# A spectral filter beside a gated feed-forward layer on one core: the first four tiles for slabs 0 and 1 alone, row parts of the weights, and stages moved in a hand-written order

## The chip, the core and the metric

The kernel runs on one core of a Trainium2 chip. A core has a matrix engine (PE) that multiplies a stationary operand of up to 128 x 128 by a moving one of up to 512 columns and adds into PSUM, a vector engine (DVE), a scalar engine with function tables (ACT), a general engine (POOL) and a queue engine (SP) that here only issues transfers. ACT and POOL issue transfers too. Each engine works through its own list in order and waits for the others through semaphores. The metric is the time of one execution in microseconds on the device, the median of several runs.

## What is computed

The input x has 2048 rows of 640 values. Its rows are normalised (mean 0, variance 1). From the normalised rows two things are made: a filter in the two-dimensional frequency domain, and a gated feed-forward layer with weights of 640 x 1536, 640 x 1536 and 1536 x 640. The result is x plus the product of both.

```
xn = _layernorm(x, axis=-1)
X  = rfft2(xn) ; X = X * (w_r + 1j * w_i) ; s = irfft2(X).astype(bfloat16)
B  = (gelu(xn @ w_gate) * (xn @ w_up)) @ w_down
return x + s * silu(B)
```

## The kernel before, in words

**Slabs and groups.** The 2048 rows are 16 slabs of 128 (slab n1 holds the rows n1, n1 + 16, ...), and four slabs are a group. `X[:, n1, :]` is a slab with its rows on the partitions. For the feed-forward layer a slab is transposed into `XG` (`xnT[g]`), 5 chunks of 128 features by 512 columns for a group. Wg, Wu hold the first two weights as 5 chunks by 1536 columns, and 128 of these columns are a tile t (12 tiles). Wd is the third weight.

**One piece of the first half of the layer** (`ffn_piece`, line 826): 5 matmuls with a tile of Wg or Wu as the stationary operand, some columns of `XG` as the moving one, into a bank of PSUM (`psg` or `psu`, two banks of each). Then ACT makes gelu of psg into `ge` (line 837), or DVE multiplies psu by `ge` into `UT` (line 839). The second half multiplies UT by Wd: `down_third` for groups 0 and 3, and for groups 1 and 2 fourteen `product`s of six matmuls with sums of blocks prepared on DVE (`w_sum`, `u_sum`).

**The order is written out by hand.** `back` (from line 1000) is a list of 144 places, each a piece of PE work; `put(s, f, ...)` hangs further work behind place s, and the last loop emits place after place. What is emitted on one engine runs there in that order. Places 0 to 15 are tiles 0 to 7 of group 0, 16 to 35 the rest of group 0, 36 to 71 group 1 (24 pieces and 12 places of products), 72 to 107 group 2, 108 to 143 group 3.

**The start.** `build` first issues transfers: slabs 0 and 1 (line 84), then Wu in pairs of tiles with slabs 2 and 3 between, and so on, all on SP and all at once (lines 94 to 106); Wg's first six tiles go out on ACT (line 231). DVE makes constants (lines 224 to 330), the last of them `a_y` (line 272). For each slab, `bn_half` twice and `bn_join` give mean and variance (lines 189, 195), a reciprocal root follows (`root_act` on ACT for slab 0, `root` with DVE's add and POOL's power for the others), and `norm` normalises in place (line 218). `slab_Tparts` transposes a slab on PE in two parts of 3 and 2 chunks and copies each from PSUM (line 995), one on DVE and one on ACT. `warm_pe(21)` stands ahead of the first transposes: matmuls of `ones` (256 columns) that nothing reads (line 588). After `root_act`'s root the table for gelu is loaded (line 215).

At place 0 slab 0 goes through tiles 0 and 1 of Wg (`GG`), slab 1 is normalised and transposed, then slab 0 goes through tiles 0 and 1 of Wu (`UU`). Place 1 does both for slab 1. Places 2 to 7 are tiles 2 to 7 for both slabs (256 columns), places 8 to 15 tiles 0 to 7 for slabs 2 and 3, and from place 16 on a piece has 512 columns. Slab 2 is transposed behind place 4, slab 3 within place 7.

**The filter.** Slabs are turned by DMA (`slab_T` with 2, line 539), folded on DVE, transformed by PE (`slab_S1`, `slab_D`) and stored to `ZDR` in DRAM. The middle stage starts when all of ZDR is written: `load_B2` (place 56, line 603) loads it in another layout, ten transfers for five bands of rows, two each. It works in 11 bursts. `s2_step(b)` at place `sb + AT[b]` does three things: PE makes `px` of burst b (line 628); PE makes `pu` of burst b - 1 (line 657); DVE and ACT sort the `pu` into RX (line 672), from where it is stored to `UDR`. Between px and pu stand ACT's copy `xs` (line 640) and DVE's two products with the filter's weights W1, W2 (line 644). `px`, `pu` and later `pv`, `pd` share two PSUM tiles. The last stage loads UDR (`load_V` at place sb + 24), gathers a few columns on POOL (line 713), transforms back (`slab_S1i`, `slab_Di`: lines 735, 762), recombines on DVE, and `finish` multiplies by silu's result, adds x and stores.

With sb = 67 the first burst's px stands behind place 67, within group 1's products.

Of the kernel before, what the change touches and what calls it, by code (L numbers as in the profile page):

```python
# [13 lines left out]
ALU = mybir.AluOpType  # L14
# [62 lines left out]
def build(nc, env):  # L77
# [5 lines left out]
    def load_x(n0, n, eng=nc.sync):  # L83
        eng.dma_start(out=X[:, n0:n0 + n, :], in_=xv[:, n0:n0 + n, :])

    def load_w(k, t0, t1, eng=nc.sync):
        f0, f1 = t0 * P, t1 * P
        eng.dma_start(out=(Wg, Wu)[k][:, :, f0:f1], in_=(wgv, wuv)[k][:, :, f0:f1])

    def load_gu(t0, t1):  # L90
        for k in range(2):
            load_w(k, t0, t1)

    load_x(0, 1)
# [9 lines left out]
    load_x(8, 4)  # L104
    nc.sync.dma_start(out=Wd, in_=B_w_down.rearrange("(t p) d -> p t d", p=P))
    load_x(12, 4)

# [104 lines left out]
    def root_act(n1):  # L212
        rstd[n1] = c1("rst0")
        nc.scalar.activation(out=rstd[n1], in_=mva[n1 // 4][:, n1 % 4, 1:2], func=ACT.Abs_reciprocal_sqrt, bias=eps)
        nc.scalar.activation(out=warm, in_=negpi, func=ACT.Gelu_apprx_tanh)

# [5 lines left out]

    ones = gtile([256], BF16)
    nc.vector.memset(ones, 1.0)
# [100 lines left out]

    fwd_consts()
    vt_iota(0)
    stats(0)
    bn_half(1, 0)
# [254 lines left out]
    def warm_pe(n):  # L584
        if not warm_bank:
            warm_bank.append(bank(0))
        for _ in range(n):
            nc.tensor.matmul(warm_bank[0][:, 0:256], lhsT=ones[:, 0:P], rhs=ones, start=True, stop=True)

# [250 lines left out]

    def ffn_part(g, t, h):
        for k in range(2):
            ffn_piece(g, t, k, h * 256, h * 256 + 256)

# [126 lines left out]

    def ffn_slab(j, tk):
        for t, k in tk:
            ffn_piece(0, t, k, j * P, j * P + P)

    GG, UU = ((0, 0), (1, 0)), ((0, 1), (1, 1))

    def run(*items):
        for it in items:
            it[0](*it[1:])  # L980

    PARTS = ((0, 3), (3, 5))

# [4 lines left out]
    def slab_Tparts(n1):  # L988
        if n1 == 0:
            xnT[0] = slot(0, 5, 512)  # L990
        for (a, b), ev in zip(PARTS, (nc.vector.tensor_copy, nc.scalar.copy)):
            pt = psB.tile([P, 5, P], BF16, tag="b")
            for c in range(a, b):
                nc.tensor.transpose(out=pt[:, c, :], in_=X[:, n1, c * P:(c + 1) * P], identity=ident)  # L994
            ev(out=xnT[0][:, a:b, n1 * P:n1 * P + P], in_=pt[:, a:b, :])
        done.add(("T", n1))

    NP = 8
    STR = (1, 2)
    back = [(run, (ffn_slab, 0, GG), (norm_parts, 1), (slab_Tparts, 1), (vt_iota, 1), (ffn_slab, 0, UU),  # L1000
             (inv_consts, 0), (inv_consts, 1)),
            (run, (ffn_slab, 1, GG + UU), (stats, 2), (root, 2, 1))]
    for h in range(2):
        for t in range(0 if h else 2, NP):
            back.append((ffn_part, 0, t, h))
        if h == 0:
            back[-1] = (run, (ffn_piece, 0, NP - 1, 0, 0, 256), (slab_Tparts, 3), (ffn_piece, 0, NP - 1, 1, 0, 256))
    for g in range(4):
# [12 lines left out]
    def put(s, *item):  # L1021
        plan[s].append(item)

    put(1, inv_rest)
    put(2, norm, 2)
    put(3, bn_half, 3, 0)
    put(4, bn_half, 3, 1)
    put(4, bn_join, 3)
    put(4, root, 3, 1)
    put(4, slab_T, 2, 1)  # L1030
    put(5, norm, 3)
    for g in range(5):
# [4 lines left out]
    for k in range(3):  # L1037
        put(9, ft_phase, 0, k)
    for k in range(4):
        put(7 + 2 * k, stats, 4 + k)  # L1040
    put(13, root, 4, 4)
    put(13, shift, 4, 4)
    for k in range(3):
        put(13, ft_phase, 1, k)
    put(12, tinv_mask, 0)
    put(14, tinv_mask, 1)
    for k in range(4):
# [133 lines left out]
```

## Time and profile before

| what | value |
|---|---|
| median of 3 runs | 193.46 us (193.43 to 193.47) |
| the profiled execution's own time | 193.65 us |
| its span (first to last recorded instruction or transfer) | 191.9 us |
| HBM read, written | 19.03 MB, 7.88 MB |
| DVE, ACT, POOL busy | 79%, 69%, 28% of the span |

A profile is of one execution. Times in it are microseconds from the start of the span. "Busy" is the time in which an engine works on an instruction; the matmuls of PE overlap, so that their ends are modelled, and PE's weight loads (PEld) run beside them. The chain of waits is followed back from the last instruction: at each step to what released it. In a timeline row stand start, duration, engine, line of the kernel, operation, output and inputs, shapes, count, and in brackets how long the engine had been idle before and what ended that. In the table by windows stand the stretch, its length, busy time and count of PE, PEld, DVE, ACT and POOL, the granted clock of PE, the mean busy share of the DMA engines and GB/s. A row of the DMA view has the transfer, the issuing queue, count, size and the median time from issue to landing.

### The profile page before, as it was taken

How to read it: one execution, taken by the hardware profiler on the slowest of the kernel's cores; microseconds unless marked ns; L12 is line 12 of the kernel's file. 1: busy time of each engine (PE TensorE's matmuls, PEld its weight loads, DVE VectorE, ACT ScalarE, POOL GpSimd, SP SyncE). 2: the span in 40 equal slices, each digit the busy share in tenths (PEclk: the TensorE clock that was granted, in tenths of full speed). 3: DMA queues.
4: the chain of work that ended last, by engine and by line, in shares of the span. 5: the costliest groups of instructions: out<-in, count | busy, mean ns of one | idle time of the engine just before them, and what ended most of it. 6: DMA issues, size and time to landing. Idle time of an engine off the chain costs nothing.

```text
span 191.9 us, 4068 instructions
## 1 busy us (share of the span) xinstructions
PE 186.1 (97%) x1453; PEld 115.6 (60%) x1469; DVE 150.9 (79%) x364; ACT 131.9 (69%) x241; POOL 53.9 (28%) x91
## 2 busy tenths in 40 slices
PE   7999999999999999999999999999999999999993
PEld 5788854677655665566543334347775555556772
DVE  6787889899799889846978677685445898888973
ACT  4658557957878778536697878634989776876622
POOL 4458768999040200000000000002030134150400
PEclk9999999999999999999999999999999999999999
DMA  6999999948889994249996444149900084778842
GB/s 164 300 329 360 370 332 170 172 99 318 178 165 191 211 300 120 78 111 230 223 108 123 106 103 103 42 107 273 266 5 0 0 117 111 152 153 213 121 174 62
DMA packets 39700, 32.43 MB, mean 169 GB/s; under 512 B 12928, under 2 KB 37760, under 8 KB 39552
## 3 DMA queue, kind: packets, MB, share of 16 engines
q1 hardware_dynamic: 35888, 27.91, 58.6%
q0 software_dynamic: 1824, 3.28, 9.4%
q10 hardware_dynamic: 1968, 0.98, 1.9%
q8 instruction: 11, 0.18, 0.4%
q14 instruction: 9, 0.07, 0.1%
HBM read 19.03 MB, written 7.88 MB: 140 GB/s over the span
## 4 chain that ended last, share of the span: by engine, by line
PE 95%; DMA 2%; DVE 1%; issue 1%; SPq 0%; ACT 0%
PE psu L832 27%; PE psg L832 27%; PE psg L967 7%; PE psg L933 7%; PE psu L967 6%; PE psu L933 5%; PE pu L657 2%; PE pd L762 2%; PE pv L735 2%; PE pz L555 2%; PE pd L573 2%; PE px L628 2%; DMA X<-in_A_x_dram 2%; PE pt L994 1%; PE pd L575 1%
## 5 line engine op out<-in xcount | busy, mean ns | idle before, releaser
L832 PE MATMUL psu<-XG,Wu 128*128 128x512 bf16 (+2 forms) x284 | 60.4, 342 | 0.5 <-issue 0.3
L832 PE MATMUL psg<-XG,Wg 128*128 128x512 bf16 (+2 forms) x280 | 60.1, 341 | 0.6
L839 DVE TENSOR_TENSOR UT<-psu,ge 128x512 bf16<-128x512 f32 (+2 forms) x58 | 34.4, 594 | 13.6 <-PE psu L832 8.1
L837 ACT ACTIVATE ge<-psg 128x512 bf16<-128x512 f32 (+2 forms) x58 | 30.3, 523 | 21.3 <-PE psg L832 20.6
L832 PEld LDWEIGHTS <-Wu 128*128 128x128 bf16 x290 | 25.9, 98 | 20.9 <-issue 3.4
L832 PEld LDWEIGHTS <-Wg 128*128 128x128 bf16 x290 | 26.5, 98 | 18.8 <-issue 0.2
L967 PEld LDWEIGHTS <-UT 128*128 128x128 bf16 x204 | 19.1, 98 | 6.9
L813 POOL DMA_DIRECT2D VY<-in_A_x_dram x12 | 10.6, 964 | 26.2 <-ACT W L737 10.5
L713 POOL COPY vr<-VY 128x128 bf16<-128x128 bf16 x2 | 0.6, 291 | 60.2 <-DMA VY<-UDR 60.2
L644 DVE TENSOR_TENSOR RZ<-xs,W 128x960 bf16<-128x960 bf16 (+2 forms) x22 | 13.3, 647 | 4.4 <-ACT xs L640 4.4
L967 PE MATMUL psg<-Wd,UT 128*128 128x320 bf16 (+1 forms) x108 | 15.7, 290 | 0.0
L578 ACT CAST RZ<-pd 128x660 bf16<-128x660 f32 x16 | 11.3, 706 | 5.2 <-PE pd L575 5.2
L189 DVE BATCH_NORM_STATS2 st<-X 128x6 f32<-128x320 bf16 x32 | 14.0, 476 | 0.6 <-DMA X<-in_A_x_dram 0.4
L933 PEld LDWEIGHTS <-UT 128*128 128x128 bf16 x120 | 11.4, 98 | 4.8 <-issue 0.4
L967 PE MATMUL psu<-Wd,UT 128*128 128x320 bf16 (+1 forms) x96 | 13.9, 293 | 0.0
L737 ACT CAST W<-pv 128x640 bf16<-128x640 f32 x16 | 11.1, 691 | 3.1 <-PE pv L735 3.1
L763 ACT ACTIVATE W<-pd 128x640 bf16<-128x640 f32 x16 | 11.3, 706 | 1.5 <-PE pd L762 1.5
L557 ACT CAST GEN<-pz 128x640 bf16<-128x640 f32 x16 | 11.2, 698 | 1.2 <-PE pz L555 1.2
L672 ACT CAST RX<-pu 128x480 bf16<-128x480 f32 (+3 forms) x22 | 10.8, 489 | 1.1 <-DVE RX L672 0.3
L640 ACT CAST xs<-px 128x960 bf16<-128x960 f32 (+2 forms) x11 | 10.3, 933 | 0.0
L207 POOL TENSOR_TENSOR rst<-ve,mhalf 128x1 f32<-128x1 f32 (+1 forms) x6 | 5.5, 913 | 11.5 <-DVE ve L205 11.5
L933 PE MATMUL psg<-X,UT 128*128 128x320 bf16 x48 | 7.8, 300 | 0.0
(202 smaller groups left out, 302.1 us busy)
## 6 DMA issues: line engine op xcount, KB each, us to landing
ZDR<-RZ SPq DMA_DIRECT2D x16, 160.5 KB, 4.1
UDR<-RX SPq DMA_DIRECT2D x10, 240.8 KB, 3.1
B<-ZDR SPq DMA_DIRECT2D x8, 240.8 KB, 5.2
W<-UDR SPq DMA_DIRECT2D x2, 963.0 KB, 9.1
X<-in_A_x_dram SPq DMA_DIRECT2D x3, 640.0 KB, 10.3
Wd<-in_B_w_down_dram SPq DMA_DIRECT2D x1, 1920.0 KB, 14.6
VY<-in_A_x_dram POOLq DMA_DIRECT2D x12, 160.0 KB, 4.3
out_dram<-VY SPq DMA_DIRECT2D x12, 160.0 KB, 2.8
```

The source lines that it names most:

```text
L189: nc.vector.bn_stats(out=st_n[n1][:, k, :], in_=X[:, n1, 320 * k:320 * k + 320])
L557: nc.scalar.copy(out=Zt[n1], in_=pz)
L578: nc.scalar.copy(out=zd.rearrange("p c (q e) -> p c q e", e=10), in_=pd[:, :, 0:330].rearrange("p c (e q) -> p c q e", q=33))
L644: nc.vector.tensor_tensor(out=pp[-1], in0=xs, in1=WT[:, :, h0:h0 + n, l0:l0 + w], op=ALU.mult)
L672: copy(out=out, in_=src)
L737: nc.scalar.copy(out=vs, in_=pv)
L763: nc.scalar.activation(out=parts(eobuf, i, 5)[:, :, n1 - DG[i][0], :], in_=pd, func=ACT.Copy, scale=(2.0 if n1 // 4 in BY_SILU else 1.0) / ...
L832: nc.tensor.matmul(ps, lhsT=WT[:, c, t * P:(t + 1) * P], rhs=xnT[g][:, c, c0:c1_], start=(c == 0), stop=(c == 4))
L837: nc.scalar.activation(out=ges[t], in_=ps, func=ACT.Gelu_apprx_tanh)
L839: nc.vector.tensor_tensor(out=UT[:, t, c0:c1_], in0=ps, in1=ges[t], op=ALU.mult)
L933: nc.tensor.matmul(ps, lhsT=lhs[:, t, :], rhs=rhs[:, t, :], start=(t == 0 and i in (0, 1, 3)), stop=(t == 5), skip_group_check=i in (2, 4, ...
L967: nc.tensor.matmul(ph, lhsT=UT[:, t, j * P:(j + 1) * P], rhs=Wd[:, t, c0:c1_], start=(t == 0), stop=(t == NT - 1))
```

## The change

- The row chunks of the weights can be loaded in parts: `PARTS = ((0, 3), (3, 5))`. ACT issues tiles 0 to 3 of Wg in two parts (before: tiles 0 to 5 in three pairs), SP tiles 0 to 3 of Wu in two parts, then tiles 4 to 7 of each in one transfer.
- Only slabs 0 and 1 are issued at once. Wu's parts stand behind a POOL copy of `a_y` into a cell of Wu; slab 2 and all later loads on SP stand behind a POOL copy of slab 0's mean into a cell of slab 2.
- `warm_pe` uses 128 columns, 38 times, and 4 times behind slab 0's transposes. The statistics' second half of slab 1, its join and its root now stand behind slab 0's normalisation and transposes; slab 1's root is made on ACT (two instructions of DVE and POOL less), and the gelu table is loaded behind it. Both copies of slabs 0 and 1 from PSUM are DVE's.
- `ffn_quad`: one slab (128 columns) through four tiles into one bank, so that one gelu or one product takes 4 x 128 columns; slabs 0 and 1 go through tiles 0 to 3 in this way (places 0 to 3). `ffn_multi`: two tiles of 256 columns into one bank: tiles 4 to 7 for slabs 0 and 1 (places 4 to 7), tiles 0 to 7 for slabs 2 and 3 (places 8 to 15). Slab 2 is transposed within place 6.
- Statistics of slabs 2 to 7 move by one place or so, `inv_consts`, `inv_rest`, norms 2 and 3 and `tinv_mask` move too.
- `sb` is 65 in place of 67: `s2_step`, `load_V`, the gathers and the whole last stage move by two places.

```
-    load_w(1, 0, 2)
-    load_w(1, 2, 4)
-    load_x(2, 1)
-    load_w(1, 4, 6)
-    load_x(3, 1)
-    load_gu(6, 8)
-    load_x(4, 4)
-    load_gu(8, 12)
...
-    for t in (0, 2, 4):
-        load_w(0, t, t + 2, nc.scalar)
+    for part in PARTS:
+        load_w(0, 0, 4, nc.scalar, *part)
...
+    nc.gpsimd.tensor_copy(out=Wu[:, 0, 0:1], in_=ab[4][0])
+    for part in PARTS:
+        load_w(1, 0, 4, nc.sync, *part)
     vt_iota(0)
-    stats(0)
+    bn_half(0, 0)
+    bn_half(0, 1)
+    bn_join(0)
+    nc.gpsimd.tensor_copy(out=X[:, 2, 0:1], in_=mva[0][:, 0, 0:1])
+    load_x(2, 1)
+    load_w(0, 4, 8)
+    load_x(3, 1)
+    load_w(1, 4, 8)
+    load_x(4, 4)
+    load_gu(8, 12)
...
     bn_half(1, 0)
     root_act(0)
...
+    def ffn_quad(k, j, *part):
+        if part[0] == 0:
+            cur["m"] = bank(k)
+        ps = cur["m"].rearrange("p (t w) -> p t w", w=P)
+        for a, b in [PARTS[i] for i in part]:
+            for i in range(4):
+                for c in range(a, b):
+                    nc.tensor.matmul(ps[:, i, :], lhsT=WT[:, c, i * P:(i + 1) * P],
+                                     rhs=xnT[0][:, c, j * P:(j + 1) * P], start=(i + c == 0), stop=(c == 4),
+                                     skip_group_check=True)
+        if part[-1] == 1:
+            multi_out(k, 0, ps, j * P, j * P + P)
...
+    def multi_out(k, t0, ps, c0, c1_):
+        if k == 0:
+            ges[t0, c0] = ge
+            nc.scalar.activation(out=ge, in_=ps, func=ACT.Gelu_apprx_tanh)
+        else:
+            nc.vector.tensor_tensor(out=UT[:, t0:t0 + n, c0:c1_], in0=ps, in1=ges[t0, c0], op=ALU.mult)
...
+    back = [(run, (ffn_quad, 0, 0, 0, 1), (vt_iota, 1)),
+            (run, (ffn_quad, 1, 0, 0), (slab_Tparts, 1), (ffn_quad, 1, 0, 1)),
+            (ffn_quad, 0, 1, 0, 1),
+            (ffn_quad, 1, 1, 0, 1)]
+    for h, k, t0 in ((0, 0, 4), (0, 0, 6), (0, 1, 4), (0, 1, 6)) + tuple((1, k, t) for t in (0, 2, 4, 6) for k in range(2)):
+        back.append((ffn_multi, k, t0, 2, 256 * h, 256 * h + 256))
+    back[6] = (run, (slab_T, 2, 1), (ffn_multi, 1, 4, 2, 0, 256))
+    back[7] = (run, (slab_Tparts, 3), (ffn_multi, 1, 6, 2, 0, 256))
...
+    put(1, stats, 2)
+    put(1, root, 2, 1)
+    put(2, bn_half, 3, 0)
+    put(2, bn_half, 3, 1)
+    put(3, norm, 2)
+    put(3, bn_join, 3)
+    put(3, root, 3, 1)
...
-    sb = 67
+    sb = 65
...
-    warm_pe(21)
+    warm_pe(38)
+    norm_parts(0)
+    slab_Tparts(0)
+    warm_pe(4)
     bn_half(1, 1)
     bn_join(1)
-    root(1, 1)
-    norm_parts(0)
-    slab_Tparts(0)
-    warm_pe(2)
+    root_act(1)
+    gelu_table()
+    norm_parts(1)
```

More of the change, by code (lines that the diff above doesn't have):

```diff
@@ L587, in warm_pe @@
         for _ in range(n):
-            nc.tensor.matmul(warm_bank[0][:, 0:256], lhsT=ones[:, 0:P], rhs=ones, start=True, stop=True)
+            nc.tensor.matmul(warm_bank[0][:, 0:P], lhsT=ones, rhs=ones, start=True, stop=True)
     st_b = {}
@@ L970, in down_third @@
                 gated(g, j, k, ph)
[L972 to L976, printed above, removed]
     def run(*items):
@@ L990, in slab_Tparts @@
             xnT[0] = slot(0, 5, 512)
-        for (a, b), ev in zip(PARTS, (nc.vector.tensor_copy, nc.scalar.copy)):
+        for (a, b), ev in zip(PARTS, (nc.vector.tensor_copy, nc.scalar.copy if n1 > 1 else nc.vector.tensor_copy)):
             pt = psB.tile([P, 5, P], BF16, tag="b")
@@ L1022, in put @@
         plan[s].append(item)
[L1024 to L1031, printed above, removed]
+    put(1, stats, 2)
[5 more added lines that the diff above has]
+    put(3, root, 3, 1)
+    put(3, inv_consts, 0)
+    put(3, inv_consts, 1)
+    put(4, inv_rest)
+    put(5, norm_parts, 3)
     for g in range(5):
@@ L1038, in build @@
         put(9, ft_phase, 0, k)
[L1039 to L1042, printed above, removed]
+    for k, at in enumerate((7, 8, 10, 12)):
+        put(at, stats, 4 + k)
+    put(12, root, 4, 4)
+    put(12, shift, 4, 4)
     for k in range(3):
         put(13, ft_phase, 1, k)
-    put(12, tinv_mask, 0)
-    put(14, tinv_mask, 1)
+    put(16, tinv_mask, 0)
+    put(18, tinv_mask, 1)
     for k in range(4):
```

47 lines of the change are left out of this document (28 added, 19 removed).

## The prediction

> **What bounds the kernel now.** I read the page first, then the chain of waits in order of time, the table by windows, and the timelines of the start and of the stage that the change moves.
>
> ```profile
> span 191.9 us, 4068 instructions
> ...
> PE 186.1 (97%) x1453; PEld 115.6 (60%) x1469; DVE 150.9 (79%) x364; ACT 131.9 (69%) x241; POOL 53.9 (28%) x91
> ...
> PE 95%; DMA 2%; DVE 1%; issue 1%; SPq 0%; ACT 0%
> ```
> ```profile
> 1.17 3.19 DMA X<-in_A_x_dram
> 4.38 0.90 DVE st L189 x2
> ...
> 6.05 0.54 PE pt L994 x5
> 6.84 0.76 PE psg L832 x10
> 7.60 0.28 PE pt L994 x5
> 7.88 0.56 PE psu L832 x10
> ...
> 9.56 0.55 PE psg L832 x5
> ...
> 187.99 0.68 PE psg L967 x12
> ...
> 188.69 0.28 ACT XG L867
> ```
> ```profile
> 6.84:188.67 181.83, 180.76 (x1425) 112.16 (x1440) 145.17 (x327) 128.19 (x235) 51.31 (x81) 1.00 0.71 170
> ```
>
> The reader is to see three pieces: a head of 6.84 us until the first real matmul, a stretch of 181.83 us in which PE is idle for 181.83 - 180.76 = 1.07 us at most, and a tail of 191.9 - 188.67 = 3.2 us behind the last matmul. The idle 1.07 us is not waiting either: the trace holds 1425 matmuls there against 1440 weight loads, and each of the 15 missing records leaves a small hole. So the middle can give nothing back. A change gains if it brings the first matmul forward or drops PE work; anything else can only add a wait. The tail hangs on the last matmuls, which the change leaves alone.
>
> **The head.** The chain shows what the first matmul waits for: the landing of slab 1, two statistics of slab 1, then the normalisation of slab 0.
>
> ```profile
> 1.18 4.55 PE L588 MATMUL psg<-GEN 128*128 128x256 bf16 x21 [1.18 <-DVE eps L229]
> ...
> 2.53 0.14 DVE L272 TENSOR_SCALAR a_y<-pb 128x1 f32<-128x1 f32 x1
> ...
> 4.05 0.21 DVE L195 BATCH_NORM_AGGREGATE mva<-st 128x2 f32<-128x12 f32 x1
> 4.29 0.29 ACT L214 ACTIVATE rst<-mva,eps 128x1 f32<-128x1 f32 x1 [2.08 <-DVE mva L195]
> ...
> 4.60 1.28 ACT L215 ACT_TABLE_LOAD   x1
> ...
> 5.62 0.63 DVE L218 TENSOR_SCALAR X<-X,mva,rst 128x384 bf16<-128x384 bf16 x2
> ...
> 6.43 0.36 DVE L995 COPY XG<-pt 128x384 bf16<-128x384 bf16 x1 [0.18 <-PE pt L994]
> ```
>
> The root of slab 0 is ready at 4.29 + 0.29 = 4.58, yet its normalisation starts at 5.62, because bn_half(1, 1), the aggregate and root(1)'s add stand before it on DVE. The change puts them behind it and leaves bn_half(1, 0) in front, which still waits for the landing at 1.17 + 3.19 = 4.36. Half of the pair's 0.90 later, at 4.83, DVE is free: **-0.79 us**. If X1 landed before the aggregate is done (4.26) it would be -0.9; if the larger pieces of Wg beside it delay it by 0.2, -0.6. I take -0.79, since X1 is issued as before.
>
> What this brings forward meets a slower PE. The 21 warm-up matmuls took 4.55 us, 217 ns for 256 columns, against 0.55 / 5 = 110 ns in the chain's row at 9.56. So 38 of 128 columns take 38 x 108 ns = 4.1 us and end at 5.28, where the transposes are now due (6.05 - 0.79 = 5.26). Three of them feed the first copy; all slow they cost 3 x (108 - 56) = 0.16 us (56 ns is 0.28 / 5 in the row at 7.60). The rate changed between 5.7 and 6.05; I take half, **+0.08**. First matmul: 6.84 - 0.71 = 6.13.
>
> [...]
>
> **PE work.** Tiles 0 to 7 were 40 matmuls of 128 columns (tiles 0, 1 for slabs 0, 1), 60 and 80 of 256; they become 80, 40 and 80. That is 40 x 56 - 20 x 110 ns (56 is 0.56 / 10 at 7.88): **+0.04**. The stage otherwise holds the same matmuls.
>
> **Weights and loads.** Wg leaves on ACT as before, in row parts. Wu's two parts now stand behind a POOL copy of a_y (2.53 + 0.14, so issued near 3.0 instead of 1.64), and X2 with all that follows on SP behind a POOL copy of mva (4.05 + 0.21, near 4.6). POOL is free for the first; before the second it has one iota, long done by then.
>
> ```profile
> 0.00:4.00 4.00, 2.82 (x14) 1.97 (x15) 2.60 (x26) 1.49 (x2) 1.98 (x9) 1.00 0.52 129
> 4.00:8.00 4.00, 3.65 (x37) 2.60 (x36) 3.11 (x12) 2.79 (x7) 0.65 (x1) 1.00 1.15 307
> 16.00:24.00 8.00, 8.00 (x77) 7.10 (x74) 6.63 (x19) 5.60 (x16) 6.54 (x5) 1.00 1.07 367
> ```
> ```profile
> Wu<-in_B_w_up_dram SPq DMA_DIRECT2D x1, 320.0 KB, 5.4
> ```
>
> By 4.0 us 129 GB/s x 4 = 0.52 MB had landed; then 307 GB/s with pieces of 512 B, 367 later with 1 KB and more. In the new order Wu part 1 ends at 1.38 MB: 4.0 + 0.86 / 0.307 = 6.8 at the slow rate (6.3 at 367). Part 2 at 1.64 MB: 7.6 (7.0). Wg 4 to 7 at 2.46 MB: 10.3 (9.3). Wu 4 to 7 at 3.28 MB: 13.0 (11.5). PE asks at 6.13 + 1.12 = 7.25, then 7.25 + 0.67 + 0.28 = 8.2, 6.13 + 80 x 0.056 + 0.28 = 10.9, and 10.9 + 4 x 0.55 + 0.28 = 13.4. All four are in time, by 0.4 to 0.6 us at the worse rate: **0**.
>
> **Statistics, table and narrow evictions.** In the new order DVE makes both copies of slab 0 (5.72 to about 6.25), then bn_half(1, 1), the aggregate, ACT's root, and norm 1 near 7.35; slab 1's transposes can start at 7.78, PE gets to them at 6.13 + 32 x 0.056 = 7.92. The copy behind them ends some **0.05** after PE wants it. gelu_table moves behind root_act(1): it ends near 7.3 + 1.28 = 8.6 where it was hidden before, so the first 512-wide gelu and its product end near 10.
>
> ```profile
> L839 DVE TENSOR_TENSOR UT<-psu,ge 128x512 bf16<-128x512 f32 (+2 forms) x58 | 34.4, 594 | 13.6 <-PE psu L832 8.1
> ```
> ```profile
> 11.27 0.56 POOL L207 TENSOR_TENSOR rst<-ve,mhalf 128x1 f32<-128x1 f32 x1 [1.44 <-DVE ve L205]
> ...
> 11.87 0.45 DVE L218 TENSOR_SCALAR X<-X,mva,rst 128x640 bf16<-128x640 bf16 x1 [0.33 <-POOL rst L207]
> ```
>
> Behind that product DVE's order is stats 2, both halves of slab 3, the second product, norm 2: 10.1 + 1.2 + 0.9 + 0.6 = 12.8, done 12.8 + 0.45 = 13.25, while PE reaches slab 2's transposes at 10.94 + 4 x 0.55 = 13.1. Slab 3 follows over POOL's power (0.56) near 14.75, PE at 14.6. These waits add to 0 (starts overlap by 0.1 each on an engine, which would clear them) to 0.3. I take **+0.10**.
>
> **The middle stage two places sooner.** Everything from the first burst on moves with sb.
>
> ```profile
> 82.94 6.26 SPq L603 DMA_DIRECT2D B<-ZDR  x10
> ...
> 87.74 0.48 DVE L875 SCALAR_TENSOR_TENSOR XG<-th,Tfwd 128x320 bf16<-128x320 f32 x1
> 87.85 0.47 ACT L870 ACTIVATE th<-FT 128x320 f32<-128x320 f32 x1 [0.61 <-DVE FT L947]
> 87.88 0.98 PE L933 MATMUL psg<-X,UT 128*128 128x320 bf16 x6
> ...
> 89.60 0.40 PE L628 MATMUL px<-B,MG 64*64 64x160 bf16 x5
> 90.35 0.97 ACT L640 CAST xs<-px 128x960 bf16<-128x960 f32 x1
> 91.41 1.24 DVE L644 TENSOR_TENSOR RZ<-xs,W 128x960 bf16<-128x960 bf16 x2 [1.52 <-ACT xs L640]
> 92.72 0.58 PE L657 MATMUL pu<-RZ,N 64*64 64x160 bf16 x10
> 94.16 0.35 DVE L672 CAST RX<-pu 128x192 bf16<-128x192 f32 x1
> 94.54 1.03 ACT L672 CAST RX<-pu 128x480 bf16<-128x480 f32 x2
> ```
> ```profile
> B<-ZDR SPq DMA_DIRECT2D x1, 240.8 KB, 4.1
> ```
>
> In the clock of before, px of burst 0 moves ahead of two products, from 89.60 to 87.97. Its second half of B (the second of the ten, issued 0.55 after 82.94) lands at 83.5 + 4.1 = 87.6: 0.4 to spare. Burst 1 now stands among the products, with two of them (6 matmuls of 320 columns each, 0.82 us at the rate of the row at 9.56) between px 1 and px 2, where one tile of 1.1 us stood as well. ACT: xs 0 at 88.4, xs 1 at 91.5 behind the tanh that needs a th buffer back; DVE: burst 0's products to 90.7, three gated writes and an add (0.48 each, less overlap), sort at 92.3; ACT's two copies out of pu 0 then end at 93.7, and PE wants that bank at 93.55. So 0.2 us of wait, at most 0.5, at least 0; **+0.10**. ACT's stores of UDR now stand on SP ahead of slabs 14 and 15's turns, which feed place 108, far behind.
>
> ```profile
> 132.42 0.29 POOL L713 COPY vr<-VY 128x128 bf16<-128x128 bf16 x1 [60.24 <-DMA VY<-UDR]
> ...
> 133.13 0.39 PE L735 MATMUL pv<-Tinv,VY 128*128 128x128 bf16 x4
> ```
>
> The inverse's first gather stood 0.7 us before its use; both move two places, the load by two tiles of 1.1, the use by two products, so its cover grows by 0.5: 0.
>
> **Sum:** -0.79 + 0.08 + 0.04 + 0 + 0.05 + 0.10 + 0.10 = -0.42. The profiled execution took 193.65 (span 191.9 and 1.75 around it), so 193.23; the runs' median, 193.46, lies 0.19 lower: **193.04 us**.
>
> **Rivals.**
> Waits eat the head: 0.3 in the early norms and 0.5 in the middle make the sum +0.18: 193.6. For it, the reckoning as it stands shows 0.45 of waits; against it, the overlap of starts.
> Weights late: if the gate on Wu delays by issue and not by bytes, part 1 lands 5.4 (the row of Wu's first load) after 3.0, at 8.4, and PE stands 8.4 - 7.25 = 1.15: -0.42 + 1.15 = +0.73, **194.2, slower**. It decides once part 1 lands after 7.25 + 0.42 = 7.7. Against it, the 5.4 held other queues' bytes.
> [...]
> The middle stands longer: if B lands 1.2 later than reckoned, its 0.4 of cover is gone and PE waits 0.8 in place of the 0.10: 193.7.
> The change doesn't do what it says: X1 lands 0.7 later beside Wg, and nothing is gained at the head: 193.7.
>
> **How the numbers follow.** Forecast 0.54, waits 0.17, late weights 0.11, slow PE 0.05, middle 0.08, X1 0.05. A measurement tells 0.2% (0.39 us) from no change. Of the forecast's own range, 192.65 (no wait at all: -0.79 + 0.04) to 193.3, about 0.44 lies under 193.07 and 0.10 above. Without the middle's wait or with a sooner X1 0.06 of the waits' case lies under it too: faster 0.50. Same: 0.10, 0.11 of the waits, 0.04 of the middle and X1: 0.25. Slower 0.25. The range for 8 in 10 runs from 192.55 (X1 at 4.26, no waits) to 194.0.
>
> **What would show it.** Right: first matmul at 6.0 to 6.3 and the last 0.3 to 0.6 sooner; norm of slab 0 at 4.83 on DVE; PE holes of 0.1 to 0.2 us before slab 3's transposes and before pu of burst 1, none before Wu's or Wg's first use. Wrong: X1 landing after 4.6, PE idle at 7.25, 8.2, 10.9 or 13.4 with a DMA as releaser, ten first matmuls in over 0.8 us, or holes between 130 and 150 us.

## The result and the profile after

| | median of 6 runs | lowest to highest | profiled execution | its span |
|---|---|---|---|---|
| before | 193.47 us | 193.42 to 193.73 | 193.65 | 191.9 |
| after | 194.33 us | 194.14 to 194.65 | 194.14 | 192.1 |

The ratio is 1.0035, with an interval of 1.0025 to 1.0046: slower by 0.86 us, where 0.42 less was forecast, and outside the range (192.55 to 194.0). The kernel before was timed again beside the changed one, so its median is of six executions here.

The page of the changed kernel: span, busy times, and the shares of the chain of waits.

```profile
span 192.1 us, 4116 instructions
...
PE 186.1 (97%) x1492; PEld 117.5 (61%) x1508; DVE 151.3 (79%) x358; ACT 130.5 (68%) x230; POOL 51.7 (27%) x92
...
PE 94%; DMA 2%; ACT 1%; issue 1%; DVE 1%; SPq 0%
```

PE is as busy as before (186.1 us). New is ACT with 1% in the chain. The chain of waits of the changed kernel over its first 17 us (start, duration, what):

```profile
1.17 3.76 DMA X<-in_A_x_dram
4.93 0.02 issue
4.96 0.50 DVE st L180
5.45 0.29 DVE X L211
5.74 0.05 issue
5.79 0.71 PE pt L1031 x5
6.50 0.24 PE psg L596 x4
6.74 1.27 PE psg L858 x20
...
13.91 0.60 ACT ge L885
14.51 0.38 ACT GEN L369
14.89 0.59 ACT XG L555
15.48 0.04 issue
15.52 0.27 PE pt L1031 x2
```

Two things stand there. X1 (slab 1) lands at 4.93 where before it landed at 4.36, so the norm of slab 0 starts only at 5.37 (the chain counts it from 5.45, where the instruction ahead of it ends) and the first real matmul at 6.74 instead of the 6.13 reckoned. And at 15.52 PE is released by ACT: slab 3's transposes wait until ACT has copied slab 2's out of PSUM (line 555), which stood behind a gelu and a phase activation (`ft_v`, line 369: a scale and an offset for the filter's phases).

The tables by windows, cut at the same marks in both kernels (span's start, first real matmul, first 512-wide matmul, last transform `pz` of the first stage, last matmul; a mark is the start of the matmul): stretch, its length, then busy times. After, then before:

```profile
0.00:6.73 6.73, 5.18 (x47) 4.79 (x48) 4.29 (x32) 1.78 (x3) 2.30 (x11) 1.00 0.74 230
6.73:25.46 18.73, 18.62 (x217) 17.16 (x216) 14.97 (x46) 11.53 (x25) 12.95 (x21) 1.00 1.06 367
25.46:76.33 50.87, 50.55 (x390) 31.31 (x394) 46.89 (x96) 38.94 (x63) 22.72 (x39) 1.00 0.88 188
76.33:188.64 112.31, 111.57 (x844) 64.20 (x852) 84.21 (x183) 77.95 (x140) 13.73 (x22) 1.00 0.56 127
```
```profile
0.00:6.84 6.84, 5.31 (x29) 3.42 (x29) 5.04 (x35) 3.48 (x6) 2.62 (x10) 1.00 0.78 203
6.84:25.24 18.40, 18.40 (x196) 16.73 (x196) 15.13 (x52) 11.83 (x33) 11.43 (x17) 1.00 1.10 347
25.24:76.11 50.87, 50.55 (x391) 31.29 (x395) 45.96 (x96) 38.78 (x64) 25.51 (x42) 1.00 0.89 201
76.11:188.44 112.33, 111.59 (x845) 64.11 (x852) 83.88 (x181) 77.58 (x140) 14.37 (x22) 1.00 0.57 127
```

After less before: head 6.73 - 6.84 = -0.11, narrow stage 18.73 - 18.40 = **+0.33**, first stage 0, the rest up to the last matmul -0.02. From the last mark the span goes on for 3.48 (before 3.43), +0.05. What lies around the span is 194.14 - 192.13 = 2.01 against 193.65 - 191.87 = 1.78, **+0.23**. Together +0.48, the difference of the two profiled executions (0.49). The medians lie 0.86 apart because before's profiled execution was 0.18 above its median and after's 0.19 below.

### The profile page after: what moved, and what is told of

It reads as the page before. It is cut to its first block, busy times and chain, and to the rows that moved or that the text cites. A ratio compares the mean times of both kernels' runs of the same rounds, so it can differ in the third digit from the quotient of the medians.

```text
span 192.1 us, 4116 instructions
## 1 busy us (share of the span) xinstructions
PE 186.1 (97%) x1492; PEld 117.5 (61%) x1508; DVE 151.3 (79%) x358; ACT 130.5 (68%) x230; POOL 51.7 (27%) x92
## 3 DMA queue, kind: packets, MB, share of 16 engines
HBM read 19.03 MB, written 7.88 MB: 140 GB/s over the span
## 4 chain that ended last, share of the span: by engine, by line
PE 94%; DMA 2%; ACT 1%; issue 1%; DVE 1%; SPq 0%
PE psu L840 23%; PE psg L840 22%; PE psg L1011 7%; PE psg L977 7%; PE psu L1011 6%; PE psu L977 5%; PE psg L874 3%; PE psu L874 3%; PE pu L665 2%; PE pv L743 2%; PE pd L770 2%; PE pz L563 2%; PE pd L581 2%; DMA X<-in_A_x_dram 2%; PE px L636 2%; PE psg L858 1%
## 5 line engine op out<-in xcount | busy, mean ns | idle before, releaser
L840 PE MATMUL psu<-XG,Wu 128*128 128x512 bf16 x194 | 49.0, 379 | 0.5 <-issue 0.3
L840 PE MATMUL psg<-XG,Wg 128*128 128x512 bf16 x190 | 48.7, 379 | 0.5
L845 ACT ACTIVATE ge<-psg 128x512 bf16<-128x512 f32 x40 | 23.9, 598 | 18.0 <-PE psg L840 17.2
L847 DVE TENSOR_TENSOR UT<-psu,ge 128x512 bf16<-128x512 f32 x40 | 27.5, 687 | 10.6 <-PE psu L840 7.0
L840 PEld LDWEIGHTS <-Wu 128*128 128x128 bf16 x200 | 18.0, 98 | 20.2 <-issue 3.2
L840 PEld LDWEIGHTS <-Wg 128*128 128x128 bf16 x200 | 18.6, 98 | 18.0
L885 ACT ACTIVATE ge<-psg 128x512 bf16<-128x512 f32 x8 | 4.8, 596 | 6.1 <-PE psg L874 5.2
L911 ACT ACTIVATE XG<-psg 128x320 bf16<-128x320 f32 (+1 forms) x11 | 4.7, 426 | 4.8 <-PE psg L1011 4.8
```

Source lines behind the costliest of these rows:

```text
L840: nc.tensor.matmul(ps, lhsT=WT[:, c, t * P:(t + 1) * P], rhs=xnT[g][:, c, c0:c1_], start=(c == 0), stop=(c == 4))
L845: nc.scalar.activation(out=ges[t], in_=ps, func=ACT.Gelu_apprx_tanh)
L847: nc.vector.tensor_tensor(out=UT[:, t, c0:c1_], in0=ps, in1=ges[t], op=ALU.mult)
```

## The experiments

Each kernel is timed against the kernel before on the same chip. "First" is the first real matmul of its profiled execution, X1 the landing of slab 1; all in us.

| run | median (lowest to highest) | ratio to before (interval) | X1 | first |
|---|---|---|---|---|
| e1 | 195.43 (195.07 to 195.91) | 1.0091 (1.0078 to 1.0105) | 5.12 | 6.76 |
| e2 | 194.69 (194.06 to 195.55) | 1.0051 (1.0029 to 1.0073) | 5.01 | 6.65 |
| e3 | 194.66 (193.94 to 195.93) | 1.0067 (1.0044 to 1.0089) | 5.24 | 6.88 |
| e4 | 194.27 (194.14 to 194.63) | 1.0033 (1.0021 to 1.0045) | 4.20 | 5.85 |
| e5 | 194.28 (194.14 to 194.50) | 1.0034 (1.0021 to 1.0048) | 4.12 | 5.83 |
| e6 | 194.47 (194.21 to 194.64) | 1.0041 (1.0029 to 1.0053) | 4.33 | 5.97 |
| e7 | 193.94 (193.76 to 194.45) | 1.0022 (1.0014 to 1.0031) | 4.06 | 6.60 |
| e8 | 194.52 (194.24 to 195.77) | 1.0067 (1.0040 to 1.0093) | 4.94 | 7.42 |
| e9 | 194.87 (194.38 to 195.55) | 1.0054 (1.0038 to 1.0070) | 4.25 | 6.73 |
| e10 | 194.76 (194.61 to 195.35) | 1.0059 (1.0045 to 1.0073) | 4.93 | 6.73 |
| e11 | 194.00 (193.92 to 194.47) | 1.0021 (1.0012 to 1.0030) | 4.13 | 6.61 |
| e12 | 195.01 (194.15 to 196.03) | 1.0068 (1.0042 to 1.0094) | 5.29 | 7.10 |
| e13 | 194.24 (194.00 to 196.31) | 1.0044 (1.0023 to 1.0064) | 5.32 | 6.97 |
| e14 | 195.27 (194.38 to 195.86) | 1.0088 (1.0065 to 1.0111) | 5.04 | 6.90 |
| e15 | 194.43 (193.91 to 195.05) | 1.0042 (1.0028 to 1.0056) | 4.74 | 6.54 |
| e16 | 193.70 (193.35 to 193.96) | 1.0003 (0.9992 to 1.0014) | 4.38 | 6.86 |

### e1: the changed kernel, Wg's row parts in pieces of two tiles

```
-        load_w(0, 0, 4, nc.scalar, *part)
+        for t in (0, 2):
+            load_w(0, t, t + 2, nc.scalar, *part)
```


> The changed kernel, with the two row parts of Wg's first four tiles each sent as two transfers of two tiles, so that a piece is 512 bytes as before and no longer 1 KB; same bytes, same queue. Theory (wide pieces of Wg take a larger share beside slab 1's transfer): slab 1 lands near 4.4 us instead of 4.93, the first real matmul starts near 6.2 instead of 6.73, and the time falls by about 0.5 us, to 193.8. Rival (the earlier issue of Wg, or the bytes as such, delay slab 1): it lands at 4.8 to 5.0 again and the time stays at 194.3.

X1 still lands late (5.12), so the size of Wg's pieces isn't what delays it. Smaller pieces only made the weights later: from the first real matmul to the first 512-wide one it took 19.63, after 18.73. The rest of its loss is at the end: four transfers on ACT instead of two make the last store signal another semaphore (see e7), and from the last landing to the end lie 1.33 instead of 0.97. A row of its timeline (start, duration, engine, line, operation; in brackets the wait):

```profile
8.79 0.83 PE L859 MATMUL psu<-XG,Wu 128*128 128x128 bf16 x12 [0.45 <-DMA Wu<-in_B_w_up_dram]
```

### e2: the changed kernel with the middle stage at its old place

```
-    sb = 65
+    sb = 67
```


> The changed kernel with sb = 67, so that the middle stage stands at its old places. Theory from the trace (PE's offset to the kernel before is 0.22 us ahead of the stage and 0.21 behind it, so that the move is worth nothing): 194.3, within 0.15. Rival (the step of the forecast: a wait of 0.1 to 0.5 at the second burst goes away): 193.8 to 194.2.

From the last transform to the last matmul it took 112.34, as before (112.33), where eleven of thirteen profiles with 65 took 112.23 to 112.25 (the changed kernel's own 112.31, e14's 112.71). So the two places gain 0.10 on PE, and are not what made the kernel slower; the runs' medians are too far spread to show 0.10.

### e3: the changed kernel, slab 3's join and root ahead of norm 2

```
-    put(3, norm, 2)
-    put(3, bn_join, 3)
-    put(3, root, 3, 1)
+    put(2, bn_join, 3)
+    put(2, root, 3, 1)
+    put(3, norm, 2)
```


> The changed kernel with slab 3's aggregate and root ahead of the second product and of slab 2's normalisation on DVE. Theory: POOL's root of slab 3 starts near 12.7 instead of 13.93, slab 3's normalisation follows slab 2's at once, PE's hole of 0.275 us within slab 3's transposes is gone, and the time falls by 0.25 to 194.1. Rival: slab 2's normalisation, pushed back by 0.3, now makes PE wait, and the time stays at 194.3.

The hole before slab 3's transposes went, and one came before slab 2's:

```profile
14.21 0.45 PE L551 MATMUL pt<-ident,X 128*128 128x128 bf16 x5 [0.18 <-DVE x_e L265]
```

PE stood some 0.35 there, since norm 2 came later. The narrow stage (first real matmul to first 512-wide one) took 18.81 against 18.73: the wait was moved, not removed, and this run does not settle its cause (e6 and e15 do).

### e4: the changed kernel with the warm-up in 256 columns

```
-    ones = gtile([128], BF16)
+    ones = gtile([256], BF16)
...
-    warm_pe(38)
+    warm_pe(19)
...
-    warm_pe(4)
+    warm_pe(2)
```


> The changed kernel with its warm-up as 19 and 2 matmuls of 256 columns instead of 38 and 4 of 128: half the instructions in the same PE time, and the longer memset puts Wg's issue on ACT back to about 1.19. Theory (the 0.3 us by which the time outside the span has grown, 2.04 against 1.75, comes with PE's additional instructions): outside the span about 1.85, the time near 194.05. Rival 1 (it has nothing to do with them): 194.3. Rival 2 (slab 1 is late because Wg was issued 0.13 us sooner): slab 1 lands near 4.5 and the time falls by 0.4 or more.

It was meant for the number of PE's instructions, 21 fewer, and that theory fell: around the span lie 2.06 (after: 2.01). But it brought X1 back. Timelines of the starts: first the kernel before, then the changed kernel, then e4:

```profile
0.72 0.86 SPq L84 DMA_DIRECT2D X<-in_A_x_dram  x2
1.19 1.01 ACTq L88 DMA_DIRECT2D Wg<-in_B_w_gate_dram  x2
```
```profile
0.82 0.17 DVE L217 MEMSET GEN<- 128x128 bf16 x1 [0.82 <-PEq L1207]
1.06 1.00 ACTq L88 DMA_DIRECT2D Wg<-in_B_w_gate_dram  x2
```
```profile
1.19 0.97 ACTq L88 DMA_DIRECT2D Wg<-in_B_w_gate_dram  x2
5.85 1.28 PE L858 MATMUL psg<-XG,Wg 128*128 128x128 bf16 x20
8.01 0.83 PE L858 MATMUL psu<-XG,Wu 128*128 128x128 bf16 x12 [0.89 <-DMA Wu<-in_B_w_up_dram]
```

SP issues X0 at 0.72 and X1 at 1.17 in all of them. Half as wide a `ones` takes DVE 0.17 instead of 0.27 to fill; `eps` behind it is ready sooner, and ACT, whose first activation reads `eps`, gets to its transfers at 1.06 instead of 1.19: Wg has slipped ahead of X1. In e4 Wg stands behind again, X1 lands at 4.20, the first matmul starts at 5.85, nearly 0.9 sooner, and then PE waits 0.89 for Wu's first part. Its first 512-wide matmul is at 25.62, after's at 25.46. In this order the early head brings nothing.

### e5: e4, with both Wg quads ahead of both Wu quads

```
-            (run, (ffn_quad, 1, 0, 0), (slab_Tparts, 1), (ffn_quad, 1, 0, 1)),
-            (ffn_quad, 0, 1, 0, 1),
+            (run, (slab_Tparts, 1), (ffn_quad, 0, 1, 0, 1)),
+            (ffn_quad, 1, 0, 0, 1),
```


> The kernel of e4_warm256 (Wg issued behind slab 1, which landed at 4.20) with the order of the four quads changed: slab 0 through Wg, slab 1's transposes, slab 1 through Wg, and only then both through Wu. Theory (in e4 the first matmul moved up to 5.85 but PE then stood 0.89 us for Wu's first part, landing at 7.88): PE asks for Wu at about 8.8 and does not wait for it, waits instead 0.3 to 0.6 for slab 1's normalisation, and the time falls by 0.3 to 0.5 to about 193.9. Rival (the loss is not at the head): 194.3.

No wait for Wu is left, but slab 1 isn't ready. Pieces of the chain of waits:

```profile
5.97 0.41 DVE st L180
...
6.98 0.39 DVE X L211
...
7.42 0.36 PE pt L1031 x3
...
7.80 0.37 DVE XG L1032
...
8.21 1.28 PE psg L858 x20
```

Second half of the statistics, root, norm, transposes and copy follow one another, and PE stands 0.48 before the transposes and 0.41 before the quad, the same 0.89. First 512-wide matmul at 25.49, and the rival's time (194.28).

### e6: e5, with norm 2 and slab 3's root sooner

```
+    put(2, norm, 2)
     put(2, bn_half, 3, 0)
     put(2, bn_half, 3, 1)
-    put(3, norm, 2)
-    put(3, bn_join, 3)
-    put(3, root, 3, 1)
+    put(2, bn_join, 3)
+    put(2, root, 3, 1)
```


> The same, and on DVE slab 2's normalisation ahead of slab 3's statistics, slab 3's aggregate and root ahead of the second product. Theory: no hole in slab 2's or slab 3's transposes, 0.3 less than e5_gate_first, near 193.5: as fast as the kernel before or 0.1 to 0.3 faster by its span, about 191.4. Rival: the same time as e5_gate_first, the hole being covered later.

The hole within slab 3's transposes stays at 0.27 (at 15.69): it isn't made by the norms. The median is 194.47, where 193.5 was expected.

### e7: the kernel before with the middle stage two places sooner

```
-    sb = 67
+    sb = 65
```


> The kernel before with sb = 65 and nothing else. Theory (the move is worth nothing): as the kernel before, within 0.15, and its time outside the span near 1.75. Rival 1 (the move costs a wait at the second burst, forecast 0.10): up to 0.5 slower. Rival 2 (the time outside the span grows with the new places): outside the span about 2.05 and 0.3 slower.

PE gains 0.10 (112.23 against 112.33), around the span lie 1.78 as before, and the time grows by 0.31. One store more (the last slabs leave in five halves instead of three) makes the last store signal another semaphore, and SP passes its last waits one after the other, some 60 ns each. When SP passed them, from the trace's semaphore events (us):

```
before  110: 190.979
e7      101: 191.338  103: .400  105: .464  106: .526  107: .585  108: .647  109: .706  110: .768
```

From the last landing to the end of the span: before 0.91, e7 1.34. 0.43 - 0.10 = +0.33, measured +0.31. (After ends on 109: 0.97.)

### e8: the kernel before, with `eps` set ahead of `ones`

```
+    eps = c1("eps")
+    nc.vector.memset(eps, 1e-5)
     nc.vector.memset(ones, 1.0)
...
-    eps = c1("eps")
-    nc.vector.memset(eps, 1e-5)
```


> The kernel before with the memset of eps put ahead of that of ones, so that ACT issues Wg before SP issues slab 1 (about 0.95 against 1.17) and not behind it (1.19); nothing else. Theory (whichever of the two queues issues first is served first): slab 1 lands 0.3 to 0.7 us later than 4.36, the first real matmul moves from 6.84 to 7.1 to 7.5, and the kernel is 0.3 to 0.6 slower. Rival (slab 1 is late in the changed kernel by the size of Wg's pieces or parts): it lands at 4.36 and the time stays.

This is the cause in question, alone. Timeline and chain of waits:

```profile
0.89 1.00 ACTq L88 DMA_DIRECT2D Wg<-in_B_w_gate_dram  x2
```
```profile
1.17 3.77 DMA X<-in_A_x_dram
4.94 0.02 issue
4.96 0.90 DVE st L189 x2
...
6.63 0.54 PE pt L994 x5
...
7.42 0.77 PE psg L832 x10
```

One memset moved, and X1 lands at 4.94 instead of 4.36, the first matmul stands at 7.42 instead of 6.84 (+0.58), and the profiled execution is 0.59 longer (194.24 against 193.65). The median is 0.89 higher, since three of its seven executions took some 195.7. The packets of the traces show the swap as well: ACT's queue (q10) starts its first one at 3.13 in the kernel before and 2.98 in e4, at 2.40 in e8 and 2.35 in the changed kernel. With e1 and e4 all four corners are measured: Wg behind X1, 4.36 with pieces of 512 B (before) and 4.20 with 1 KB (e4); Wg ahead, 4.94 and 5.12 with 512 B (e8, e1) and 4.93 with 1 KB (after). The order decides; the size makes no difference that shows in these five profiles.

### e9: the kernel before with a warm-up of 128 columns

```
-            nc.tensor.matmul(warm_bank[0][:, 0:256], lhsT=ones[:, 0:P], rhs=ones, start=True, stop=True)
+            nc.tensor.matmul(warm_bank[0][:, 0:P], lhsT=ones[:, 0:P], rhs=ones[:, 0:P], start=True, stop=True)
...
-    warm_pe(21)
+    warm_pe(42)
-    warm_pe(2)
+    warm_pe(4)
```


> The kernel before with its warm-up as 42 and 4 matmuls of 128 columns instead of 21 and 2 of 256 (46 rows more in PE's program, the same PE time; the memset of ones, and so Wg's issue, stay). Theory (the time outside the span, 1.78 in three profiles of the kernel before and its variants, 1.91 to 2.13 in seven of the changed kernel and its variants, comes with PE's additional instructions at the start): outside the span 2.0 and the time 0.25 longer, near 193.9. Rival: outside the span 1.78, the time stays at 193.6.

`ones` keeps its 256 columns here, and X1 its landing (4.25). The profiled execution (195.55) had a wait of 0.92 for Wu at 15.56, and 2.66 around its span: a block of 16 KB of the program was fetched at 194.6, behind the span's end at 192.9. So neither expectation holds: the time around the span grew, but by 0.88 and not by 0.2, and the median by 1.26 (194.87 against 193.61). Of that the profile shows the wait and the time around the span; whether the additional rows of PE's program cause either is not shown.

### e10: the changed kernel with three phase activations one place later

```
-        put(3 + g, ft_v, g)
+        put(3 + g + (g > 1), ft_v, g)
```


> The changed kernel with three of ACT's phase activations (ft_v of bands 2 to 4) one place later, so that ACT's copy of slab 2's transposes stands ahead of the third and not behind it. Theory (slab 3's second part needs the bank that slab 2's transposes hold until ACT has copied them): the copy starts 0.4 sooner, at 14.4, PE's hole of 0.275 within slab 3's transposes is gone, and the time falls by 0.25. Rival (the hole hangs on slab 3's normalisation, as forecast): the hole stays and so does the time. In e3_slab3_root slab 3's root was sooner and slab 2's normalisation later: there the hole moved ahead of slab 2's transposes, which fits either.

Timeline rows: ACT's copy of slab 2's transposes, slab 3's transposes on PE, and a later wait.

```profile
14.73 0.69 ACT L555 COPY XG<-pt 128x640 bf16<-128x640 bf16 x1
16.10 0.44 PE L1031 MATMUL pt<-ident,X 128*128 128x128 bf16 x5
34.16 1.24 PE L840 MATMUL psu<-XG,Wu 128*128 128x512 bf16 x5 [0.23 <-DVE UT L847]
```

Slab 3's five transposes run in 0.44, without the hole (0.72 in the changed kernel). This run alone doesn't show the cause, since PE had stood 0.53 for Wu ahead of 15.00 and came to slab 3 only after the copy had ended (14.73 + 0.69 = 15.42); e15 settles it. And PE now waits at 34.16 for a product that frees its bank: from the first 512-wide matmul to the first transform it took 16.64, where the changed kernel took 16.24. With the wait for Wu the narrow stage took 19.48. The median is not better.

### e11: the kernel before with one load more

```
-    load_x(12, 4)
+    load_x(12, 2)
+    load_x(14, 2)
```


> The kernel before with the load of slabs 12 to 15 in two transfers, so that one more transfer comes ahead of the last store and the store's semaphore is the next in the rotation (101 in place of 110). Theory (at the end SP waits for the transfers' semaphores one after the other, some 0.06 us each, and those that stand behind the last store's are still ahead of it when it lands): from the last landing to the span's end 1.34 us instead of 0.91, the time 0.4 longer, near 194.05. This would also explain e7_before_sb65, whose last store had semaphore 101. Rival (that kernel was slower for its middle stage): the time stays at 193.6.

+0.39 in the median, with no edit to the middle stage: the last store again signals 101, and from its landing to the end lie 1.34. This is e7's explanation, alone.

### e12: the changed kernel without the two gates

```
-    nc.gpsimd.tensor_copy(out=Wu[:, 0, 0:1], in_=ab[4][0])
...
-    nc.gpsimd.tensor_copy(out=X[:, 2, 0:1], in_=mva[0][:, 0, 0:1])
```


> The changed kernel without the two POOL copies behind which Wu's first part and slab 2 with all later loads stand: SP issues all of them at once. Theory (DMA is full from 3 us on and SP's queue is worked off in order, so that the gates change nothing that PE waits for): slab 1 at 4.9, the time 194.3 within 0.2. Rival 1 (the gates delay Wu): Wu's first part lands 0.5 or more sooner, no gain in this order of quads. Rival 2 (Wu's pieces beside Wg and slab 1 crowd them out): slab 1 or Wg later, 0.3 or more slower. If the gates are what lengthens the time outside the span, that falls to 1.8.

Four executions took 194.15 to 194.47, four 195.55 to 196.03. The profiled one is of the second kind; its PE rows:

```profile
6.15 0.71 PE L1029 MATMUL pt<-ident,X 128*128 128x128 bf16 x5 [0.88 <-DVE X L211]
7.10 2.33 PE L856 MATMUL psg<-XG,Wg 128*128 128x128 bf16 x20
```

Twenty matmuls in 2.33 us where the changed kernel's row has 1.28: PE ran at half rate until 10.2, which costs (10.2 - 7.1) / 2 = 1.55, and the narrow stage took 20.24 against 18.73. Without the gates the better executions are as long as the changed kernel's: the gates are not what costs. Nor do they make the time around the span, which is 2.07.

### e13: the changed kernel with 16 small instructions more on DVE and on ACT

```
+    pads = (c1("pad_v"), c1("pad_a"))
+
+    def pad():
+        nc.vector.memset(pads[0], 0.0)
+        nc.scalar.copy(out=pads[1], in_=b_0)
+    for k in range(16):
+        put(100 + 2 * k, pad)
```


> The changed kernel with 16 small memsets on DVE and 16 small copies on ACT added in the last third of the span, on engines that wait for PE there. Theory (in the trace of the changed kernel two blocks of 8 KB of program are fetched 1.1 and 1.9 us behind the span's end, in the kernel before the same two at 176.4 and 186.6 us: DVE's and ACT's programs have become shorter by some instructions, and the fetch of their last block now falls into the end): the two fetches fall before the span's end, the time outside the span goes from 2.0 to 2.15 back to 1.8, and the time falls by 0.25 in spite of 32 more instructions. Rival (the time outside the span depends on something else): 2.05 again, 194.3 or more.

DVE's recorded program grew from 447 to 463 and one of the two blocks (DVE's, it seems) was fetched at 182.1, well inside the span; ACT's did not grow (16 waits fewer beside 16 copies more), and the other block still came behind the end. 1.95 around the span, after 2.01; the median is that of the changed kernel (194.24 against 194.33). So the run tests only one half of the theory, and moving one of the two blocks did not bring 1.8.

### e14: the changed kernel with a longer warm-up

```
-    warm_pe(38)
+    warm_pe(46)
```


> The changed kernel with 46 warm-up matmuls ahead of slab 0's transposes instead of 38. Theory (since slab 1 lands late, PE stands idle for 0.7 to 1.2 us between warm-up and transposes, and in part of the executions its rate then rises only after 9 us, as in the profile of e12_no_gates, which costs 1.3 us: the runs of 195.5 to 196.0 in e2, e3, e8 and e12): no execution above 195.2, the median 194.3 to 194.6 (the transposes wait up to 0.2 for the warm-up). Rival (the idle time has nothing to do with it): one run in three to four near 195.6 again.

The theory that an unbroken warm-up brings the rate sooner fell: it rose near 6.7 (after: 6.4), and three of six executions took 195.3 to 195.9, where none above 195.2 was expected.

### e15: the changed kernel with the edits of e4, e5, e6, e10 and e13

> The changed kernel with all that the runs so far speak for: Wg issued behind slab 1 and both quads of Wg first (e5), norms and roots of slabs 2 and 3 sooner (e6), ACT's copy of slab 2's transposes ahead of the third phase activation (e10), and the additional instructions of e13_pad. Theory (the causes add): e5's 194.28 less 0.27 less 0.25, near 193.75, the span near 191.8. If a cause is still missing: 194.2 or more. It is not expected to beat the kernel before by what can be measured, since PE still stands 0.9 us for slab 1 behind the first quad.

194.43 instead of 193.75. The waits for slab 1 (0.46 and 0.41) and at 33.89 (0.42) stand as in e5 and e10: cures of single waits, each of which shows the next.

The hole's cause, though, is shown here. Timeline rows of the changed kernel, then of e15 (ACT's copy of slab 2's transposes, slab 3's transposes):

```profile
14.79 0.68 ACT L555 COPY XG<-pt 128x640 bf16<-128x640 bf16 x1
15.08 0.72 PE L1031 MATMUL pt<-ident,X 128*128 128x128 bf16 x5
```
```profile
15.14 0.69 ACT L555 COPY XG<-pt 128x640 bf16<-128x640 bf16 x1
15.82 0.44 PE L1031 MATMUL pt<-ident,X 128*128 128x128 bf16 x5
```

Slab 2's transposes start at 13.71 and 14.45, so slab 3's follow by 1.37 in both, but the copy by 1.08 and by 0.69. With the copy sooner the hole is gone. In e6, with the same norms and roots, the distances are 1.37 and 1.08, and the hole is there.

### e16: the kernel before, sooner middle stage, more loads

```
-    sb = 67
+    sb = 65
...
-    load_x(4, 4)
+    for n in range(4, 8):
+        load_x(n, 1)
...
-    load_x(8, 4)
+    for n in range(8, 12):
+        load_x(n, 1)
...
-    load_x(12, 4)
+    load_x(12, 2)
+    load_x(14, 2)
```


> The kernel before with sb = 65 and the loads of slabs 4 to 15 in ten transfers instead of three, so that the last store's semaphore comes last in SP's final waits again (110). Theory (the middle stage two places sooner gains 0.10 of PE's time, from the last transform to the last matmul 112.23 instead of 112.33, and e7_before_sb65 lost 0.43 at the end by its last semaphore): from the last landing to the end 0.91, the time 0.1 below the kernel before, 193.5. Rival (the finer loads cost as much or more): 193.6 to 193.9.

The last store signals 110 again, the end takes 0.92, PE's gain of 0.10 is there, and a third block of 8 KB, it seems of SP's program, which is nine instructions longer, is fetched behind the end (193.7): 1.93 around the span. The sum is nothing: 1.0003. No version beat the kernel before.

## Why the prediction was wrong

**The head, -0.79: this step failed**, at its reason "since X1 is issued as before". X1 is, Wg isn't. The cause is a line of the diff that the listing above leaves out:

```
-    ones = gtile([256], BF16)
+    ones = gtile([128], BF16)
```

The step counted what the narrower `ones` does to PE. It did not count that DVE now fills it 0.10 us faster, that `eps` behind it is set sooner, and that ACT's transfers wait for `eps`: Wg leaves at 1.06, ahead of X1 at 1.17, and no longer at 1.19. e8 and e4 show it from both sides. X1 came 0.57 later (4.93, past the 4.6 that the prediction named as a sign of being wrong), and norm 0 started at 5.37, 0.25 sooner and not 0.79. Its row and that of the copy it leads to, from the timeline of the changed kernel:

```profile
5.37 0.62 DVE L211 TENSOR_SCALAR X<-X,mva,rst 128x384 bf16<-128x384 bf16 x2
...
6.32 0.56 DVE L1032 COPY XG<-pt 128x384 bf16<-128x384 bf16 x2 [0.34 <-PE pt L1031]
```

The rival with X1 beside Wg had the effect (0.7 reckoned) and a chance of 0.05, but no mechanism. The only one named, in the head's paragraph, is the larger pieces of Wg, which e1 and e8 rule out. The rival of the late weights came nearest in time (194.2), by luck: the changed kernel waits for no weight.

**Slow transposes, +0.08:** from the first of them to the copy 6.32 - 5.79 = 0.53 against 6.43 - 6.05 = 0.38, so the full +0.15; the rate rose near 6.4, not before. -0.79 + 0.54 + 0.15 gives the measured -0.11 within rounding. What sets the moment of the rise, no run shows: in the profiles, with matmuls from 1.04 to 1.21 on, the time from one matmul to the next halved at 3.9 (e13, 2.9 us after the first matmul) to 6.8 (e10), and in e12 at 10.2; in the changed kernel it fell from 107 to 56 ns at 6.40. The windows' clock column doesn't tell it: for the changed kernel's first 6.73 us it shows 1.00, though its matmuls started 107 ns apart until 6.40. Slow PE, 0.05 among the chances, did not come in the changed kernel (its first twenty real matmuls start 56 ns apart); it came in e12's profile.

**Weights, 0:** right for the changed kernel, which waits for none. Yet the reckoning was wrong, and only the late head hid it: part 1 was put at 6.8 by the bytes ahead of it; it landed at 7.2, in e4 at 7.88, and PE in e4 wanted it at 7.13. Transfers that SP issued later (Wu's second part, slabs 2 and 3, Wg 4 to 7, Wu 4 to 7, from 3.39 to 5.92 in e4) shared the engines with it: by its landing in e4 the packets had moved 1.81 MB, where it and all ahead of it are 1.38. The sum by bytes took them to be served in order. So had X1 come as reckoned, PE would have waited for weights as in e4 (0.89), which is the effect of the rival with a chance of 0.11, and e5 shows slab 1's own chain right behind it. In e4, e5, e6 and e15 the first matmul came at 5.83 to 6.54, and nothing of it was left at the first 512-wide one (25.49 to 25.92, before 25.24).

**Narrow matmuls and the copy, +0.09:** 0.33 less the hole leaves 0.05 for both.

**Norms 2 and 3, +0.10:** a wait of 0.27 stood at slab 3's transposes, as said, but not for the norm (e6). It was for a PSUM bank: ACT's list had the copy out of it behind a gelu and a phase activation (the chain of waits; e15 against e6). The step listed DVE's order place by place and never ACT's.

**Middle, +0.10:** the wait before pu of burst 1 didn't come, and the two places gain 0.10 in eleven of thirteen profiles with 65 (e2, e7). The sign was wrong. The changed kernel's own profile shows only 0.02 of it because of a small wait further on, at the inverse's first gather:

```profile
131.34 0.29 POOL L721 COPY vr<-VY 128x128 bf16<-128x128 bf16 x1 [59.93 <-DMA VY<-UDR]
...
131.93 0.23 PE L743 MATMUL pv<-Tinv,vr 128*128 128x128 bf16 x1
```

The gathers waited for VY, which landed at 131.22, and PE lost 0.08 to the second of the first pair (131.58 to 131.87). The prediction gave this place 0, with cover growing by 0.5 over the 0.7 of before; from the first gather to the first `pv` it is 0.30 here (131.34 to 131.64) and 0.87 in e3. And e14's 112.71 is a small case of the rival with a late B: the second half of the first band landed at 88.81 (after: 88.01), and a gap of 0.37 within the first burst's px ended at 88.86, right behind it.

**What the sum did not have:** +0.05 behind the last matmul (the last store on semaphore 109), and +0.23 around the span. For the second there is a candidate, the fetches of the program itself, which have queues of their own. The changed kernel's rows of its page (12 packets of 16 KB and 7 of 8 KB), then the blocks fetched last, from the trace:

```profile
q8 instruction: 12, 0.20, 0.5%
q14 instruction: 7, 0.06, 0.1%
```
```
kernel    last fetches (us: KB)      span's end   around the span
before    176.4: 8   186.6: 8        191.87       1.78
e7        175.8: 8   182.0: 8        192.67       1.78
after     193.2: 8   194.0: 8        192.13       2.01
e4        193.3: 8   194.1: 8        192.21       2.06
e9        187.7: 8   194.6: 16       192.89       2.66
```

DVE's program went from 459 to 447 recorded instructions and ACT's from 334 to 315, which would fit if the last blocks, fetched within the span before, are now needed only behind its end. Over the profiles the tie holds: 1.78 to 1.81 around the span without such a block (before, e7, e8, e11), 1.91 to 2.66 with one or more; e2, with 1.92 and none seen, is against it. That the block is the cause isn't shown, since e13 moved only one of the two.

**Open:** executions over 195.3. Eight of the nine versions in which Wg leaves ahead of X1 had some, all but the changed kernel itself with its six runs; of the nine with Wg behind only e9 had one, and the kernel before in 26 runs beside e13 to e16 none above 194.45. So they go with the order of issue, by this count over versions; how is not shown: the profiled ones have a late rate (e12) or late weights (e9, e10), and neither the gates (e12) nor the warm-up's length (e14) is what brings them.

## What to carry to other kernels

An edit to a warm-up or to a constant is also an edit to every queue whose first transfer waits behind it (here ACT's left 0.13 us sooner, and X1 landed 0.57 later): before a gain at the head is counted, write down in which order the queues issue their first transfers, to 0.1 us. When one input comes sooner, the next may become the wait: before the gain is taken, follow the next two inputs (here Wu's first part and slab 1's statistics) to the same mark. And an end that is fixed has parts that a diff moves unseen: the semaphore of the last store (up to 0.43 us here), and perhaps where the last block of the program falls (0.1 to 0.9 us).

## What was not expected of the hardware

- Two transfers on two queues: with Wg issued 0.02 us behind X1, X1 landed at 4.06 to 4.74 in nine profiles; with Wg ahead by 0.11 or 0.28, at 4.93 to 5.32 in another nine. No profile lies between. ACT's queue started its first packet at 2.88 to 3.16 in the former and at 2.28 to 2.47 in the latter, so 0.13 us at the issue became 0.4 or more at the first packet.
- A final wait on a semaphore that was signalled long before still costs SP some 60 ns, in the order of the semaphores: 0.91 us from last landing to the end where the last store has the last semaphore, 1.33 to 1.34 where it has the first (e1, e7, e11).
- Taking instructions out of DVE's and ACT's programs went with a longer time around the span (2.01 instead of 1.78); the cause is open.
